# A gated mix of linear attention and a GLU on one core: half of the gates' logits taken from the transposed x, the rest behind the query folds; sums stored by rows; diagonals built at the load

## The chip, the core and the metric

The kernel runs on one core of a Trainium2 chip. TensorE (PE) multiplies, VectorE (DVE) and ScalarE (ACT) work on data in on-chip memory, SyncE (SP) and GpSimd (POOL) here only issue DMAs. The metric is the time of one execution on the device in microseconds (us); three runs of a kernel give a median.

## The reference: what is computed

```python
x = A_x                                            # 2048 x 1024, float32
g = sigmoid((x * gate_w).sum(-1, keepdims=True))   # the gates: one logit per token
a = _A_ref(x, A_wqkv, A_w_phi, A_wo)               # linear attention, 32 heads of 32
b = _B_ref(x, B_w_gate, B_w_up, B_w_down)          # (gelu(x @ w_gate) * (x @ w_up)) @ w_down
return g * a + (1 - g) * b
```

In `_A_ref` queries and keys go through a per-head 32x32 map `w_phi`; the features are softmax(p) and softmax(-p) side by side, 64 to a head. Two sums over all keys, `kv` (features times values) and `z` (features alone), finish the key side; each query then gives `num / den`, and `wo` follows.

## The kernel before, in words

**Tiling.** Everything is float32, split into a high and a low part (`high` on ACT, `low` on DVE), and each product is made of three passes on PE. Large products use a seven-product block scheme (Strassen-Winograd form): sums of quarters of x and of weights are formed first, on DVE. Tokens come in two halves of 1024. The first pool runs 79 units of seven steps; a step is twelve 128x512 matmuls (`product`, L748, L755). First come seven units for keys and values of half 1, then half 0's keys and values, half 0's gate, up and query columns, and from `second_turn` on the same columns for half 1, with kept weights. The last stage (L1456) multiplies by `wo` and `w_down`.

**Folds.** `w_phi` is folded into the key and query weights: `key_fold` and `query_fold` multiply a 128-row piece of the weights by a block-diagonal 128x128 matrix that `diagonal` (L473) builds on DVE. The eight query folds (L944 to L974) load `wqT` into one of two buffers (`into`), build the diagonal in one of two places, put eight products, which the trace shows as 16 matmuls, between two steps as a "filler", copy the result on ACT and store it from POOL to `wq_fold`.

**The sums of x for half 0.** `late_sums` (L246) loads chunk `kc` of two token blocks of the transposed x (`x_load`, rows `kc` and `kc + 4` of eight groups of 128 features), makes four sums on DVE (`x_sums`) and stores them from POOL in `xs_late`. Chunks 1 and 3 belong to `first_part` and use the `pts` tile (`raw`); chunks 0 and 2 belong to `second_part` and use `extra[2]` and `extra[3]`, two of four parts of the tile `work`.

**The gates.** `gates` (L919) runs in `second_part`, after its late sums: gate_w is broadcast to all rows (`extra[0]`), the 16 blocks of 128 rows of x are loaded in turn into `extra[2]` and `extra[3]` (SP, L925), one DVE instruction with an accumulator makes each block's logits (L933), and a sigmoid on ACT and two small DVE instructions follow (L938 to L941). After that the same three parts take the pieces of x for the first turn (`pieces`, `x_convert`; L276). They go in fixed order through the three buffers, and only when they are through may the features start (`entered`); `first_part`'s query folds must be done too (`prepared`).

**Features, finish, attention.** 32 jobs of `features` (L979) load keys and values, transpose (L1001), form the softmax and add to `kv` through a filler (L1052). `finish` (L1068) reads the 32 partial sums, adds, transposes and stores them in `sums_of` (L1108) with four DMAs on SP; `attention` (L1124) then works on the queries in the background of the units.

**The order of the work** is written by a planner inside the kernel. Each stream of work is a generator that yields requests (engine, length, ready time, due step); `run` (L191) picks, ahead of each PE step, what can start before it, the earliest start first, then the earliest due step. Lengths and landing times are constants (`LAND` 5.0, `STORE` 4.5, a step 2.73). The order it finds is fixed in each engine's queue: at run time an instruction waits in its queue for its data, and all behind it wait too. A DMA on SP waits in SP's queue likewise.

Of the kernel before, what the change touches and what calls it, by code (L numbers as in the profile page):

```python
# [8 lines left out]
F32 = mybir.dt.float32  # L9
F32R = mybir.dt.float32r  # L10
AF = mybir.ActivationFunctionType
OP = mybir.AluOpType
# [4 lines left out]
P = 128  # L17
KC = D // P
NF = DF // P
NG = H // 4  # L20
# [11 lines left out]
def tile_gated_mix(ctx: ExitStack, tc: tile.TileContext, x, xT, wkT, wqT, wv, w_phi, wo,  # L32
# [100 lines left out]
    with tc.tile_pool(name="xa", bufs=1) as xa, tc.tile_pool(name="fp", bufs=1) as fp, \  # L133
# [112 lines left out]
        def late_sums(half, which, r1, r2, free):  # L246
            for kc in which:
                end = yield SYN, LAND + 2.0, free, INF
                x_load(half, kc, r1, r2)
                steps = x_sums(r1, r2)  # L250
                for part in (0.75, 0.75, 1.5):
                    end = yield VEC, part, end, now[0] + 8
                    next(steps, None)
                for k, t in enumerate((r2[:, BLK:], r1[:, :BLK], r2[:, :BLK], r1[:, BLK:])):
                    nc.gpsimd.dma_start(xs_late[half][k][:, kc, :], t)
                free = end + STORE + 1.0
            return free
# [191 lines left out]
                    f"p ({' '.join(names)}) -> p {' '.join(names)}", **dict(zip(names[1:], shape[1:])))  # L449

        tails = fp.tile([P, 256], F32, name="tails")

        def new_f(dtype):
            return fp.tile([P, 1024], dtype, tag="f", name="f", bufs=1)
# [24 lines left out]
        work = new_quarter(0, 0).rearrange("p a b c -> p (a b c)")  # L479
        gated = [[work.bitcast(F32)[:, (2 * j + m) * BLK:(2 * j + m + 1) * BLK] for m in range(2)] for j in range(2)]  # L480
        extra = [work.bitcast(F32)[:, 1024 * k:1024 * k + 1024] for k in range(4)]
        raw_in = work[:, 3072:]
        EARLY = 12
        spare = new_weight(F32).rearrange("p i a b -> p (i a b)")
# [191 lines left out]
        highs((1, 2), (1, 3))  # L676
        for k, _ in stages[:4]:
            held[k] = 0.0

        raw_free = [INF, INF, INF]  # L680

# [208 lines left out]
        def first_part():  # L890
            yield SYN, 0.0, lambda: raw_free[2], INF
            raw = xa.tile([P, 2, 2 * BLK], F32, tag="pts", name="raw", bufs=1)
            pts_free[0] = INF
            into = [raw[:, 0], raw[:, 1]]
            free = yield from late_sums(0, (1, 3), *into, 0.0)
            yield from query_folds(into, free)
            pts_free[0] = max(folded[g] for g in range(NG))
            places[0].blocks = new_f(F32R).rearrange("p (b c) -> p b c", c=P)
            prepared[0] = 0.0

        def second_part():
            free = yield from late_sums(0, (0, 2), extra[2], extra[3], lambda: folded["k"])
            free = yield from gates([extra[2], extra[3]], extra[0], free)
            ends_of = []

            def turned(end):
                ends_of.append(end)
                if len(ends_of) == 2:
                    entered[0] = max(ends_of)
            start(pieces(first_turn, 0, extra[2], (0, 4), free, turned))  # L910
            start(pieces(first_turn, 0, extra[3], (1, 5, 9, 11, 13), free, turned))
            start(pieces(first_turn, 0, extra[0], (2, 6, 8, 10, 12), free))
            start(ring_pieces(first_turn, 0, (3, 7)))
# [2 lines left out]
            p = places[0]  # L916
            return max(p.free, p.attended, other_free[0])

        def gates(into, gw, free):  # L919
            yield SYN, LAND, free, INF  # L920
            nc.sync.dma_start(gw, gate_w[None, :].to_broadcast([P, D]))
            landed = []

            def load(c, at):
                nc.sync.dma_start(into[c % 2], x[c * P:(c + 1) * P, :])  # L925
                landed.append(at + 5.2)

            for c in range(2):
                load(c, free + c)
            for c in range(S // P):  # L930
                end = yield VEC, 1.25, lambda c=c: landed[c], now[0] + 6
                s = into[c % 2]
                nc.vector.scalar_tensor_tensor(s, s, 1.0, gw, op0=OP.mult, op1=OP.mult, accum_out=logit[:, c:c + 1])  # L933
                if c + 2 < S // P:
                    load(c + 2, end)
            out = end
            end = yield SCA, 0.3, end, now[0] + 6, "sigmoid"
            nc.scalar.activation(g_a, logit, AF.Sigmoid)  # L938
            yield VEC, 1.2, end, now[0] + 6
            nc.vector.tensor_scalar(g_b, g_a, -1.0, 1.0, OP.mult, OP.add)  # L940
            nc.vector.tensor_scalar(g_n, g_a, 1.0, -1.0, OP.mult, OP.add)  # L941
            return out

        def query_folds(into, free):  # L944
            free = [free] * 2
            for g in range(NG):
                s = into[g % 2]
                landed = yield SYN, LAND + 6.0, lambda: free[g % 2], INF
                nc.sync.dma_start(s, wqT[g])
                free[g % 2] = INF  # L950
                end = yield VEC, 0.3, landed, now[0] + 6
                bp = query_diagonals[g % 2]
                diagonal(bp, g)
                fillers.append((lambda end=end: max(end, misc_free[0]), query_fold(g, s, bp, free), 1.9))
            yield SYN, 0.0, lambda: max(free), INF

        def query_fold(g, s, bp, free):
# [110 lines left out]
        def finish(p):  # L1068
            landed = yield SYN, LAND + 7.0, lambda: max(max(kept), place_free(), v_free[0], pts_free[0]), INF
            z, other = tails[:, :64], tails[:, 64:P]  # L1070
            p.second(new_f(F32)[:, :1024])
            raw = xa.tile([P, 2, 2 * BLK], F32, tag="pts", name="raw", bufs=1)
            pts_free[0] = INF
            chunks, total = [*p.wide, raw[:, 0], raw[:, 1]], raw_in.bitcast(F32)
            for c, t in enumerate(chunks):
                nc.sync.dma_start(t.rearrange("p (u n) -> p u n", n=2 * P), kv_parts[:, 4 * c:4 * c + 4])
            soon = lambda: now[0] + 3
            yield VEC, 1.1, 0.0, soon()
            nc.vector.tensor_tensor(z, z, other, OP.add)
            for at in (32, 96):  # L1080
                nc.vector.tensor_copy(other[at - 32:at], z[at:at + 32])
            nc.vector.tensor_tensor(z[:96], z[:96], other[:96], OP.add)
            nc.vector.tensor_copy(other[:32], z[64:96])
            nc.vector.tensor_tensor(z[:32], z[:32], other[:32], OP.add)
            nc.vector.transpose(other[:32], z[:32])
            for q in range(4):
                nc.gpsimd.dma_start(sums_of[32 * q:32 * q + 32, 1].rearrange("b u d -> u b d"),
                                    other[16 * (q % 2):16 * (q % 2) + 16, 32 * (q // 2):32 * (q // 2) + 32]
                                    .unsqueeze(1).to_broadcast([16, 32, 32]))
            for c, t in enumerate(chunks):  # L1090
                end = yield VEC, 0.85, landed + 1.5 * c, now[0] + 12
                for h in range(2):
                    rows = slice(64 * h, 64 * h + 64)
                    e = t[rows].rearrange("p (u e s h f) -> p e h u s f", u=4, e=2, s=2, h=2)[:, :, h]
                    nc.vector.tensor_tensor(total[rows, 256 * c:256 * c + 256].rearrange("p (u s f) -> p u s f", u=4, s=2),
                                            e[:, 0], e[:, 1], OP.add)
            pts_free[0] = end
            end = yield VEC, 1.27, end - SIGNAL, soon()
            nc.vector.transpose(p.wide[0], total)
            moved = yield SCA, 2.2, end, soon()  # L1100
            rows = [slice(64 * h, 64 * h + 32) for h in range(2)]
            for h in range(2):
                nc.scalar.activation(p.wide[1][rows[h]], p.wide[0][64 * h + 32:64 * h + 64], AF.Copy)
            end = yield VEC, 2.5, moved, soon()
            for h in range(2):
                nc.vector.tensor_tensor(p.wide[1][rows[h]], p.wide[0][rows[h]], p.wide[1][rows[h]], OP.add)
                for s in range(2):
                    nc.sync.dma_start(sums_of[64 * s + 32 * h:64 * s + 32 * h + 32, 0],  # L1108
                                      p.wide[1][rows[h]].rearrange("p (u s d) -> p s u d", s=2, d=32)[:, s])
            yield VEC, 1.6, end - SIGNAL, soon()  # L1110
            for h in range(4):
                for q in range(4):
                    nc.vector.tensor_copy(g_at[32 * h:32 * h + 32, :, q], g_a[32 * q:32 * q + 32, :])
            p.parts = {n: raw_in.bitcast(F32)[:, at:at + size] for n, at, size in
                       (("kz", 0, 128), ("kb", 128, 128), ("mm", 256, 32), ("st", 288, 96))}
            p.free = sums_ready[0] = end + STORE + 8.0

        def load_query(p, half, g, j):
            nc.sync.dma_start(p.e[:64], heads["q"][half][g][j].rearrange("(w r) t -> r w t", w=2))
# [425 lines left out]
```

## Time and profile before

| | us |
|---|---|
| median of three runs | 2341.13 (2337.79 to 2342.32) |
| the profiled execution | 2341.17 |
| its span, first to last instruction | 2339.3 |
| PE busy | 2315.9 (99%) |
| DVE busy | 1811.5 (77%) |
| ACT busy | 1111.0 (47%) |
| POOL busy | 380.2 (16%) |

Rows of the timeline give start, length, engine, line, operation and what is written from what; in brackets the idle time before it and what ended it. `SPq` rows are DMA issues in SP's queue: their length is how long they held the queue, waits between them included where several are merged (x2). A row of windows gives a stretch, its length, then busy time and number of instructions of PE, PEld (weight loads), DVE, ACT and POOL, then PE's granted clock, the share of DMA engines busy and GB/s. Tiles go by their names in the program: `x` covers `work` and its parts, `f` the constants and later other uses, `tyz` and `wgu` weights, `misc` the folds' results.

### The profile page before, as it was taken

Reading aid. Unit: us, or ns where it says so; the run is one execution under the profiler, and the core shown is the slowest. Engines: PE = TensorE matmul, PEld = TensorE weight load, DVE = VectorE, ACT = ScalarE, POOL = GpSimd, SP = SyncE. Lnnn points to the kernel's source line nnn. Section 1 sums busy time; section 2 is a strip of 40 time slices with the busy share of each in tenths; the row PEclk is TensorE's granted clock in tenths of the full one; section 3 lists DMA queues with packets and bytes.
Section 4 is the critical chain, followed back from the end, with each engine's and each line's share of the span. In section 5 each row is a group of like instructions: output and inputs, shape, how many; then the busy total and the mean of one; then the engine's idle time right before and its main releaser. Section 6 shows DMA issues by size and latency. Waiting matters only on the chain.

```text
span 2339.3 us, 29314 instructions
## 1 busy us (share of the span) xinstructions
PE 2315.9 (99%) x10408; PEld 1921.2 (82%) x10408; DVE 1811.5 (77%) x2402; ACT 1111.0 (47%) x1496; POOL 380.2 (16%) x646
## 2 busy tenths in 40 slices
PE   8999999999999999999999999999999999999999
PEld 7778888888888888878888888888888888888887
DVE  7655898888988888878899888872674868867774
ACT  6435555565555656555566655652433332223221
POOL 3211111111222122222323222232000000000000
PEclk9999999999999999999999999999999999999999
DMA  9888548888889889898888888886784767978773
GB/s 340 298 286 293 162 150 291 308 307 312 315 297 330 302 285 318 285 301 245 249 239 261 233 246 251 236 252 212 275 283 153 262 241 267 325 255 314 267 264 134
DMA packets 238610, 622.33 MB, mean 266 GB/s; under 512 B 31936, under 2 KB 69568, under 8 KB 222592
## 3 DMA queue, kind: packets, MB, share of 16 engines
q1 hardware_dynamic: 149360, 308.47, 40.4%
q0 software_dynamic: 87904, 311.73, 39.9%
q8 instruction: 82, 1.34, 0.2%
q14 instruction: 64, 0.52, 0.1%
q10 hardware_dynamic: 1200, 0.26, 0.1%
HBM read 413.79 MB, written 206.57 MB: 265 GB/s over the span
## 4 chain that ended last, share of the span: by engine, by line
PE 92%; DMA 4%; issue 2%; DVE 1%; ACT 1%; POOL 0%; SPq 0%; DVEq 0%; POOLq 0%; ACTq 0%
PE po L1456 29%; PE a L755 25%; PE c L755 17%; PE b L755 9%; PE p L755 8%; PE misc L1052 1%; PE misc L1211 1%; DMA stage<-wk 1%; DMA raw<-in_xT 1%; DMA stage<-in_wv 1%; DMA x<-in_xT 0%; PE misc L962 0%; DMA stage<-xs 0%; DMA wk<-stage 0%; DMA xs<-x 0%
## 5 line engine op out<-in xcount | busy, mean ns | idle before, releaser
L1456 PE MATMUL po<-tw,wgu 128*128 128x512 f32 x1344 | 309.8, 389 | 0.0
L1456 PEld LDWEIGHTS po<-tw,wgu 128*128 128x128 f32 x1344 | 252.3, 188 | 52.3
L116 ACT ACTIVATE wgu<-stage 128x1024 fp32r<-128x1024 f32 x130 | 137.5, 1058 | 305.2 <-PE po L1456 227.8
L119 DVE TENSOR_TENSOR wgu<-stage,wgu 128x1024 fp32r<-128x1024 f32 x130 | 158.6, 1220 | 127.8 <-ACT wgu L116 127.7
L755 PE MATMUL c<-x,tyz 128*128 128x512 f32 x948 | 228.8, 390 | 4.1 <-ACT c L772 3.4
L755 PE MATMUL b<-s,tyz 128*128 128x512 f32 x948 | 229.6, 391 | 2.3 <-ACT b L783 2.3
L755 PE MATMUL a<-s,v 128*128 128x512 f32 x948 | 228.3, 389 | 1.5 <-DVE s L119 0.8
L755 PE MATMUL c<-x,wgu 128*128 128x512 f32 x948 | 228.7, 390 | 0.9 <-DVE x L119 0.6
L755 PE MATMUL a<-x,wgu 128*128 128x512 f32 x948 | 228.6, 390 | 0.8 <-DVE h L739 0.8
L755 PE MATMUL a<-s,tyz 128*128 128x512 f32 x948 | 228.4, 389 | 0.2 <-DVE tyz L119 0.2
L755 PE MATMUL p<-s,tyz 128*128 128x512 f32 x948 | 228.1, 389 | 0.0
L755 PEld LDWEIGHTS c<-x,tyz 128*128 128x128 f32 x948 | 177.3, 188 | 42.6 <-ACT c L772 5.0
L755 PEld LDWEIGHTS b<-s,tyz 128*128 128x128 f32 x948 | 178.0, 189 | 39.8 <-ACT b L783 3.1
L755 PEld LDWEIGHTS a<-s,v 128*128 128x128 f32 x948 | 177.8, 188 | 38.9 <-ACT s L116 1.2
L755 PEld LDWEIGHTS a<-x,wgu 128*128 128x128 f32 x948 | 178.1, 188 | 38.5 <-DVE h L739 1.2
L755 PEld LDWEIGHTS c<-x,wgu 128*128 128x128 f32 x948 | 177.1, 188 | 37.9 <-DVE x L119 1.0
L755 PEld LDWEIGHTS a<-s,tyz 128*128 128x128 f32 x948 | 177.4, 188 | 37.0 <-DVE tyz L119 0.7
L755 PEld LDWEIGHTS p<-s,tyz 128*128 128x128 f32 x948 | 177.4, 188 | 36.4
L1456 PE MATMUL po<-tw,wl 128*128 128x512 f32 x672 | 156.9, 389 | 0.0
L1456 PE MATMUL po<-tyz,wgu 128*128 128x512 f32 x672 | 155.2, 389 | 0.0
L1456 PEld LDWEIGHTS po<-tw,wl 128*128 128x128 f32 x672 | 126.2, 188 | 26.2
L1456 PEld LDWEIGHTS po<-tyz,wgu 128*128 128x128 f32 x672 | 126.2, 188 | 26.2
(442 smaller groups left out, 3561.0 us busy)
## 6 DMA issues: line engine op xcount, KB each, us to landing
stage<-lm SPq DMA_DIRECT2D x98, 512.0 KB, 3.6
sr<-in_w_down SPq DMA_DIRECT2D x84, 512.0 KB, 5.8
sl<-lm SPq DMA_DIRECT2D x70, 512.0 KB, 4.5
lm<-h POOLq DMA_DIRECT2D x112, 256.0 KB, 4.5
stage<-in_w_gate SPq DMA_DIRECT2D x28, 512.0 KB, 7.0
stage<-in_w_up SPq DMA_DIRECT2D x28, 512.0 KB, 5.8
stage<-la SPq DMA_DIRECT2D x28, 512.0 KB, 4.8
sr<-in_wo SPq DMA_DIRECT2D x20, 512.0 KB, 5.8
```

Source lines behind the costliest of these rows:

```text
L116: nc.scalar.activation(dst, src, AF.Copy)
L119: nc.vector.tensor_tensor(dst, src, dst_h.bitcast(F32), OP.subtract)
L755: nc.tensor.matmul(dst, w[:, h, 4 * part + kc, :], xq[:, e, kc, :], start=first and kc == 0 and i == 0, stop=kc == 3 and i == 2, skip_grou ...
L1052: nc.tensor.matmul(po[:, :2 * P], blocks[:, b], pts[:, b].rearrange("p e q f -> p (e q f)"), start=b == 0, stop=b == 7, skip_group_check=True)
L1211: nc.tensor.matmul(po[s], kbs[:, s].rearrange("p a b -> p (a b)"), pts[:, q, s, :], start=q == 0, stop=q == 1)
L1456: nc.tensor.matmul(ps[c], ls[:, a, m, c * P:(c + 1) * P], rs[:, e, m], start=opens and m == 0 and j == 0, stop=closes and m == 1 and j == 2)
```

## The change

`late_sums` now also makes dots: for each loaded block (token block `j`, features `kc` and `kc + 4`) two DVE instructions add feature times gate weight into `dots`, 128 partitions by 1024 tokens, which is `extra[0]`. The gate weights come as columns (`gate_columns`, 128 x 8) by a new DMA on SP at the end of the prologue. `second_part` then calls `first_logits`: `dots` is transposed in 32x32 blocks, reduced, moved across partitions by 16 small copies and reduced again to the first eight columns of `logit`. The other eight blocks of rows are done by `second_logits`, called in `first_part` behind the query folds, with the folds' buffers and a new `f` tile; its loads are requested at most one in two steps. The sigmoid follows there, and `prepared` is set after it.

In `query_folds` the diagonal is requested at once after the load is issued, no longer when the load has landed; the filler keeps waiting for the landing. In `finish` the last addition writes `total` in the order of the stored rows, so that a store's row is one run of 512 elements instead of 16 runs of 32, and the planner counts the sums as ready 3 us after `STORE` in place of 8.

```diff
@@ late_sums @@
                 x_load(half, kc, r1, r2)
+                for r, j in ((r1, 1), (r2, 0)):
+                    yield VEC, 1.5, end, now[0] + 8
+                    for a in range(2):
+                        at, c = slice(BLK * j, BLK * j + BLK), kc + 4 * a
+                        s, gate_c = r[:, BLK * a:BLK * a + BLK], gate_columns[:, c:c + 1]
+                        if j in dotted:
+                            nc.vector.scalar_tensor_tensor(dots[:, at], s, gate_c, dots[:, at], op0=OP.mult, op1=OP.add)
+                        else:
+                            nc.vector.tensor_scalar(dots[:, at], s, gate_c, 0.0, OP.mult, OP.add)
+                            dotted.add(j)
                 steps = x_sums(r1, r2)
...
+        gate_columns, dotted = tails[:, P:P + 8], set()
...
+        dots = extra[0]
...
+        nc.sync.dma_start(gate_columns, gate_w.rearrange("(c p) -> p c", p=P))
@@ first_part @@
             yield from query_folds(into, free)
-            pts_free[0] = max(folded[g] for g in range(NG))
+            free = max(folded[g] for g in range(NG))
+            end = yield from second_logits([into[1], new_f(F32)], into[0], free)
+            pts_free[0] = end
             places[0].blocks = new_f(F32R).rearrange("p (b c) -> p b c", c=P)
+            yield from gates(end)
             prepared[0] = 0.0
@@ second_part @@
-            free = yield from gates([extra[2], extra[3]], extra[0], free)
+            free = yield from first_logits(extra[2], extra[3], free)
...
+        def first_logits(t, r, free):
+            end = yield VEC, 1.27, free, now[0] + 8
+            nc.vector.transpose(t, dots)
+            end = yield VEC, 1.25, end - SIGNAL, now[0] + 8
+            nc.vector.tensor_reduce(r[:, :32], t.rearrange("p (b i) -> p b i", i=32), AX.X, OP.add)
+            end = yield VEC, 2.2, end - SIGNAL, now[0] + 8
+            parts = r[:, 32:64].rearrange("p (a c) -> p a c", a=4)
+            for a in range(4):
+                for q in range(4):
+                    nc.vector.tensor_copy(parts[32 * q:32 * q + 32, a], r[32 * a:32 * a + 32, q:32:4])
+            nc.vector.tensor_reduce(logit[:, :8], parts.rearrange("p a c -> p c a"), AX.X, OP.add)
+            return end
+
+        def second_logits(into, gw, free):
             yield SYN, LAND, free, INF
             nc.sync.dma_start(gw, gate_w[None, :].to_broadcast([P, D]))
+            landed, first, end = [], now[0] + 1, 0.0
+            for c in range(8, 16):
+                at = yield SYN, LAND, lambda: max(free if c < 10 else end, begun(first + 2 * (c - 8))), INF
                 nc.sync.dma_start(into[c % 2], x[c * P:(c + 1) * P, :])
+                landed.append(at)
+                if len(landed) == 2:
+                    end = yield VEC, 1.25, landed.pop(0), now[0] + 6
+                    dot(into[(c - 1) % 2], gw, c - 1)
+            end = yield VEC, 1.25, landed.pop(0), now[0] + 6
+            dot(into[1], gw, 15)
+            return end
@@ query_folds @@
-                end = yield VEC, 0.3, landed, now[0] + 6
+                end = yield VEC, 0.3, 0.0, now[0] + 6
                 bp = query_diagonals[g % 2]
                 diagonal(bp, g)
-                fillers.append((lambda end=end: max(end, misc_free[0]), query_fold(g, s, bp, free), 1.9))
+                fillers.append((lambda end=max(end, landed): max(end, misc_free[0]), query_fold(g, s, bp, free), 1.9))
@@ finish @@
             for h in range(2):
-                nc.vector.tensor_tensor(p.wide[1][rows[h]], p.wide[0][rows[h]], p.wide[1][rows[h]], OP.add)
+                by_s = [w[rows[h]].rearrange("p (u s d) -> p s u d", s=2, d=32) for w in p.wide]
+                out = total[rows[h]].rearrange("p (s u d) -> p s u d", s=2, d=32)
+                nc.vector.tensor_tensor(out, by_s[0], by_s[1], OP.add)
                 for s in range(2):
                     nc.sync.dma_start(sums_of[64 * s + 32 * h:64 * s + 32 * h + 32, 0],
-                                      p.wide[1][rows[h]].rearrange("p (u s d) -> p s u d", s=2, d=32)[:, s])
+                                      out[:, s])
...
-            p.free = sums_ready[0] = end + STORE + 8.0
+            p.free = sums_ready[0] = end + STORE + 3.0
```

`dot` is the old loop's instruction (L933), and the new `gates` holds only the sigmoid and the two instructions after it.

More of the change, by code (lines that the diff above doesn't have):

```diff
@@ L917, in place_free, with dot, gates @@
             return max(p.free, p.attended, other_free[0])
-        def gates(into, gw, free):
+        def first_logits(t, r, free):
[11 more added lines that the diff above has]
+        def second_logits(into, gw, free):
             yield SYN, LAND, free, INF
             nc.sync.dma_start(gw, gate_w[None, :].to_broadcast([P, D]))
-            landed = []
-            def load(c, at):
+            landed, first, end = [], now[0] + 1, 0.0
+            for c in range(8, 16):
+                at = yield SYN, LAND, lambda: max(free if c < 10 else end, begun(first + 2 * (c - 8))), INF
                 nc.sync.dma_start(into[c % 2], x[c * P:(c + 1) * P, :])
[L926 to L936, printed above, removed]
+                landed.append(at)
[5 more added lines that the diff above has]
+            return end
+        def dot(s, gw, c):
+            nc.vector.scalar_tensor_tensor(s, s, 1.0, gw, op0=OP.mult, op1=OP.mult, accum_out=logit[:, c:c + 1])
+        def gates(end):
             end = yield SCA, 0.3, end, now[0] + 6, "sigmoid"
@@ L941, in gates @@
             nc.vector.tensor_scalar(g_n, g_a, 1.0, -1.0, OP.mult, OP.add)
-            return out
         def query_folds(into, free):
@@ L1105, in finish @@
             for h in range(2):
-                nc.vector.tensor_tensor(p.wide[1][rows[h]], p.wide[0][rows[h]], p.wide[1][rows[h]], OP.add)
+                by_s = [w[rows[h]].rearrange("p (u s d) -> p s u d", s=2, d=32) for w in p.wide]
+                out = total[rows[h]].rearrange("p (s u d) -> p s u d", s=2, d=32)
+                nc.vector.tensor_tensor(out, by_s[0], by_s[1], OP.add)
                 for s in range(2):
-                    nc.sync.dma_start(sums_of[64 * s + 32 * h:64 * s + 32 * h + 32, 0],
-                                      p.wide[1][rows[h]].rearrange("p (u s d) -> p s u d", s=2, d=32)[:, s])
+                    nc.sync.dma_start(sums_of[64 * s + 32 * h:64 * s + 32 * h + 32, 0], out[:, s])
             yield VEC, 1.6, end - SIGNAL, soon()
```

## The prediction

> **What bounds the kernel now.** I read the page first, for span and chain.
>
> ```profile
> span 2339.3 us, 29314 instructions
> PE 92%; DMA 4%; issue 2%; DVE 1%; ACT 1%; POOL 0%; SPq 0%; DVEq 0%; POOLq 0%; ACTq 0%
> ```
>
> TensorE (PE) is the bound and works on nearly all the time, so an edit that adds or removes no matmul can gain only where PE stands still or runs at a lower clock. The profiled execution took 2341.17 us, 1.9 us around its span, and the median of the runs is 2341.13: the sum is made against 2341.2. Next, PE's waits in three stretches: 100 to 200, 200 to 1000 and 1000 to 1100 us (after 1100 there are none). Columns: total, times, longest.
>
> ```profile
> PE misc L962 <- issue: 3.9, 1, 3.9
> PE c L755 <- ACT c L772: 3.0, 2, 2.7
> PE a L755 <- DVE h L739: 0.8, 1, 0.8
> PE b L755 <- ACT b L783: 0.5, 1, 0.5
> ...
> PE a L755 <- DVE s L119: 0.8, 1, 0.8
> PE a L755 <- ACT s L116: 0.7, 1, 0.7
> PE c L755 <- DVE x L119: 0.7, 1, 0.7
> ...
> PE b L755 <- ACT b L783: 1.8, 1, 1.8
> PE c L755 <- DVE x L119: 0.6, 1, 0.6
> ```
>
> These 12.8 us are nearly all that can be won. Two stalls also cost clock (windows; PEclk is the number before the DMA share):
>
> ```profile
> 172.00:178.00 6.00, 5.94 (x27) 5.55 (x28) 5.96 (x9) 1.98 (x4) 0.38 (x1) 0.72 0.59 215
> 1020.60:1028.00 7.40, 7.33 (x25) 5.90 (x26) 4.53 (x5) 3.59 (x6) 3.62 (x6) 0.77 0.82 261
> ```
>
> **Part 1: the gates leave the early stretch.** The old loop sends 16 loads of x rows through SP's queue; each waits there for the dot product that frees its buffer, and the weight loads stand behind it. SP's queue, what SP waited for (60 to 260 us), and the vector engine (DVE) and PE in time:
>
> ```profile
> 157.82 5.87 SPq L925 DMA_DIRECT2D x<-in_x  x2
> 163.79 0.56 SPq L43 DMA_DIRECT2D stage<-wk  x1
> ...
> SPq L925 <- DVE x L933: 45.2, 13, 7.9
> ...
> 170.34 0.69 DVE L97 TENSOR_TENSOR stage<-stage 128x512 f32<-128x512 f32 x1 [5.59 <-DMA stage<-wk]
> 171.68 0.28 DVE L474 TENSOR_TENSOR f<-f 128x128 f32<-128x128 f32 x1
> ...
> 172.06 3.65 PE L962 MATMUL misc<-f,raw 128*128 128x128 f32 x16 [3.87 <-issue]
> 186.46 1.95 PE L962 MATMUL misc<-f,raw 128*128 128x128 f32 x16
> ```
>
> This is the 3.9 us stall from end to end: the x-row loads held SP for 5.87 us, the weight load went out at 163.79, DVE stood 5.59 us for it, the fold's diagonal (L474) was queued behind on DVE, and PE behind the diagonal. The change cuts it twice: the loads are gone from there, and the diagonal is issued at the load instead of at the landing. Removed: 3.87 of idle, and 3.65 − 1.95 = 1.70 of slow clock: **−5.6**. The 0.8, 0.5 and 0.3 (3.0 − 2.7) of the same stretch are work of the same queues behind dots and late weights: **−1.6**. What is late next there is the landing of wqT itself, which is requested when its buffer is free and not changed in size.
>
> The eight dots and eight loads that are left, with one broadcast of gate_w, now follow the folds, at some 190 to 240 us by the planner's spacing of two steps (5.4 us) a load. There SP carries the first-turn pieces of x, and DVE their conversions. A load that waits for a late dot would again hold weights and pieces; between 0 and the 5.6 of the stall above. The new loop asks for a load after the dot that frees its buffer, so I take the row nearest to this, two small stalls of 0.8: **+1.6**.
>
> **Part 2: the first-turn pieces start earlier.** Their three buffers were the gates'.
>
> ```profile
> 183.71 0.43 SPq L276 DMA_DIRECT2D stage<-xs  x1
> ...
> 229.85 1.48 SPq L276 DMA_DIRECT2D x<-xs  x2
> ```
>
> The first piece went out just after the last dot, the last two only at 229.85, and PE then waited 0.8 + 0.7 + 0.7 for conversions. Free sooner (the planner lets the first piece go eleven steps ahead of its half's first unit), the chain through the buffers gets ahead of its uses: **−2.2**; at worst 0. The first half of the logits needs a transpose, two reductions and 16 small copies on DVE after the late sums; at most some 7 us (1.25 each for transpose and reduction by the first row below, 16 copies of 32 rows by at most the 0.28 of L474), in place of 16 × 1.22 = 19.5 of dots taken from the same stretch: 0.
>
> ```profile
> L1001 DVE STREAM_TRANSPOSE x<-x x32: 1235/1245/1247, 241.9 to 948.5; 128x1024 f32<-128x1024 f32 x32
> L933 DVE SCALAR_TENSOR_TENSOR x<-x x16: 1212/1219/1226, 120.9 to 181.4; 128x1024 f32<-128x1024 f32 x16
> ```
>
> **Part 3: finished sums by rows.** SP's queue at the second turn, the stores' own durations in ns (least, median, most), and the chain's pieces on PE:
>
> ```profile
> 1001.67 6.90 SPq L1108 DMA_DIRECT2D sums<-f  x4
> 1008.68 2.55 SPq L276 DMA_DIRECT2D stage<-in_xT  x1
> ...
> L1108 SPq DMA_DIRECT2D sums<-f x4: 319/1970/2509, 1001.7 to 1006.1; - x4
> ...
> 1020.66 4.30 PE b L755 x12
> ```
>
> Each store writes 32 rows in 16 pieces of 128 bytes; after the first, which found the queue empty, each held it about 2 us, and the load of the x piece behind them another 2.55. Stored as 32 runs of 2 KB, all four should take about the least, 4 × 0.32 = 1.3 instead of 6.90: the piece goes out 5.6 us earlier. PE's wait for its conversion (0.6) and for ACT's copy behind the next pieces (1.8) are both shorter than 5.6 and should go, with 1.4 of slow clock (4.30 for a group of twelve that takes 2.88 in the row of 92.32 below): **−3.8**. DVE's addition only changes its access order, at the same count.
> The Trainium skill (TensorE: Matmul & The Clock Gate, Part 1: The HAM clock gate) says that PE falls to half clock after an idle window of about 3.4 us, windows that run freely. Here 0.77 was granted after 0.6 + 1.8 of idle in two parts; by the rule on the length alone part 3 would be worth −2.4 and the sum 1.4 less (an estimate). The row decides.
>
> **Part 4: the dots beside the late sums.** Four chunks get four instructions each of 128x512 on DVE, 16 in all, ahead of each chunk's sums.
>
> ```profile
> L240 DVE TENSOR_TENSOR x<-x x2: 691/692/692, 88.2 to 108.2; 128x512 f32<-128x512 f32 x2
> 60.00:100.00 40.00, 39.63 (x181) 32.53 (x181) 27.78 (x37) 16.55 (x25) 11.71 (x21) 1.00 0.89 285
> ...
> 90.87 1.22 DVE L119 TENSOR_TENSOR tyz<-stage,tyz 128x1024 fp32r<-128x1024 f32 x1
> 92.32 2.88 PE L755 MATMUL a<-s,tyz 128*128 128x512 f32 x12
> ...
> 97.02 1.24 SPq L233 DMA_DIRECT2D x<-in_xT  x2
> 98.31 0.60 SPq L43 DMA_DIRECT2D stage<-in_wv  x1
> ...
> 108.26 0.63 ACT L116 ACTIVATE v<-stage 128x512 fp32r<-128x512 f32 x1 [6.02 <-DMA stage<-in_wv]
> ```
>
> By L240's 0.69 that is 2.76 us a chunk, 11 in all, into a stretch whose DVE is busy 27.78 of 40 (a mean, that hides queues). The low half of the z weights ended at 92.09 for a matmul at 92.32: slack 0.2. If the dots go ahead of it, PE waits about 2.76 − 0.2 = 2.5; there are two such chunks (88.2 and 108.2 us), so the loss is up to 5.0. The planner takes the earlier due time among ready work, and dots have eight steps. On the other side, chunks end 3 us later, so the x load of 97.02 may fall behind the wv load of 98.31, whose late landing held ACT for 6.02 and, behind it, the copy for which PE stood the 2.7 above: that would be −2.7. Between −2.7 and +5.0 I take one late z: **+2.5**.
>
> **Part 5: the column load of gate_w.** 1,024 elements of 4 bytes, each alone in DRAM, at 43.6 us on SP.
>
> ```profile
> L43 SPq DMA_DIRECT2D stage<-in_wv x1: 1480/1480/1480, 43.6 to 43.6; - x1
> ...
> DMA to landing us min/median/max: 9.8/9.8/9.8
> ...
> 57.42 1.05 ACT L116 ACTIVATE wgu<-stage 128x1024 fp32r<-128x1024 f32 x1
> ```
>
> From above: twice the pieces of a sums store at 2.5, so 5.0 of the queue; from below 0.3. The weight load behind it landed at 43.6 + 9.8 = 53.4 and was used at 57.42, so 4.0 is covered: between 0 and +1.0. I take 0.
> The Trainium skill (DMA: Bandwidth & Descriptors, Rules for kernel authors) speaks against this edit: a last dimension that is not contiguous becomes one descriptor per element. By it the upper end, +1.0, would hold (an estimate), and the sum be −8.1.
>
> **Not on the path.** Features start when both the pieces and now the logits are done, so a few us later or as before; their end and attention's leave slack: 1600:1650 has DVE at 15.10 of 50 before the last stage. The sums are counted ready 5 us sooner: nothing waits there.
>
> ```profile
> 1600.00:1650.00 50.00, 50.00 (x222) 41.44 (x221) 15.10 (x18) 12.88 (x19) 8.41 (x14) 1.00 0.54 175
> ```
>
> Sum: −5.6 − 1.6 + 1.6 − 2.2 − 3.8 + 2.5 = −9.1, so 2341.2 − 9.1 = **2332**.
>
> **Rivals.** PE's matmuls of the query folds, first and last:
>
> ```profile
> L962 PE MATMUL misc<-f,raw x128: 270/275/485, 117.1 to 213.5; 128*128 128x128 f32 x128
> ```
>
> (a) The SP hold comes back: an x-row load of the second half waits for a late dot, with weights behind it. For it: 45.2 us of such waits in the old loop. Against: half the loads, issued after the dots. It costs 5.6 in place of 1.6, so −5.1: 2336.
> (b) The stores by rows don't help, since the finish has moved away from the second turn, or the pieces wait for ring buffers anyway: −9.1 + 3.8 = −5.3, 2336. For it: the planner's order is made anew. Against: the first transpose of the features at 241.9 is near where I expect the new one.
> (c) Slower: the features start late. Their start now waits for eight loads at two steps each, 14 steps or 38 us (14 × 2.7) behind the last fold's store. If the folds don't speed up (the last was at 213.5), that is past 251, and the finish with its reads, stores and DVE work falls on the second turn's conversions. From a delay of some 20 us the 3.8 isn't won and, by two more stalls like that one, 7.6 is lost: −9.1 + 3.8 + 7.6 = +2.3, 2343.5, and +6.1 with a third.
> (d) Better: z is never late, the wv load passes the x load, the x rows never hold SP: −9.1 − 2.5 − 2.7 − 1.6 = −15.9, 2325.
>
> **Chances.** Forecast 0.43 (2329.5 to 2335), (a) 0.16, (b) 0.13, (c) 0.18, (d) 0.10. About 0.2%, 4.7 us, is what a measurement of this kernel tells from no change. (a) and (b) lie at −5.1 and −5.3, on that edge, half each way: faster 0.43 + 0.10 + 0.15 = 0.68. (c) starts at +2.3; two thirds of it beyond +4.7: slower 0.12, and the same 0.20. The range goes from (d) to (c), 2325 to 2344.
>
> **What would show it.** The wait of L962 on issue gone, no L925 in SP's queue between 117 and 183 us; SP's four sums stores under 2 us and clock 1.00 after 1020; no wait of L755 on x or s conversions near 231. Wrong, if L755 waits for L119 near 90 or 112 us (part 4), if the new loads hold SP for 5 us (a), if the first features' transpose is past 260 us (c).

## The result, and the profile after

The changed kernel takes 2325.78 us (median of six runs, 2323.88 to 2328.37); the kernel before, run beside it, 2340.66 (2337.01 to 2342.32). The ratio is 0.9938, with a 95% interval of 0.9926 to 0.9951: 14.5 us less, between 11.5 and 17.3. The forecast was 9.1 us less, 2332; the time lies at the good end of the range, 0.8 us inside it and next to rival (d)'s 2325. The profiled execution took 2328.37, the longest of the six, and has a span of 2326.6, 12.7 less than before's 2339.3.

The page after, span and chain:

```profile
span 2326.6 us, 29294 instructions
PE 94%; DMA 3%; DVE 1%; ACT 0%; issue 0%; SPq 0%; DVEq 0%; ACTq 0%
```

The chain runs over PE for 94% where it was 92%. PE's waits in the changed kernel, the stretch of 50 to 100 us first and that of 300 to 600 us behind it; from 100 to 300 and from 600 on there are none:

```profile
PE c L768 <- ACT c L785: 2.2, 2, 1.9
PE c L768 <- ACT c L789: 0.3, 1, 0.3
PE a L768 <- DVE tyz L119: 0.2, 1, 0.2
...
PE a L768 <- ACT c L789: 0.9, 1, 0.9
PE a L768 <- DVE h L742: 0.7, 1, 0.7
```

Of the 12.8 us of waits that the prediction listed, none is left; 3.5 us stand elsewhere (1.9 + 0.9 + 0.7). The stretch of the old gates' loop, in windows of the kernel before and then of the changed one (PE busy is the second number):

```profile
117.00:185.00 68.00, 62.35 (x304) 51.87 (x303) 41.86 (x66) 24.37 (x39) 8.68 (x16) 0.97 0.82 286
```

```profile
117.00:185.00 68.00, 68.00 (x350) 58.08 (x350) 37.97 (x63) 30.19 (x45) 12.45 (x23) 1.00 0.72 248
172.00:178.00 6.00, 6.00 (x35) 5.17 (x34) 2.15 (x3) 4.00 (x7) 1.08 (x2) 1.00 0.62 241
1000.00:1050.00 50.00, 50.00 (x226) 41.55 (x225) 29.94 (x57) 22.55 (x31) 15.81 (x26) 1.00 0.96 309
```

PE went from 304 matmuls in these 68 us to 350, without a gap and at full clock, and the second turn (1000 to 1050 us, 47.55 busy before) has no gap either. SP's queue in the changed kernel, at the first pieces, the late rows of x, and the second turn:

```profile
44.45 0.48 SPq L691 DMA_DIRECT2D tails<-in_gate_w  x1
...
94.22 0.37 SPq L43 DMA_DIRECT2D stage<-in_wv  x1
...
107.23 0.88 SPq L233 DMA_DIRECT2D x<-in_xT  x2
...
156.45 1.93 SPq L286 DMA_DIRECT2D x<-in_xT  x2
...
210.31 1.19 SPq L954 DMA_DIRECT2D raw<-in_x  x1
...
1006.41 1.56 SPq L286 DMA_DIRECT2D stage<-xs  x2
...
1013.85 0.32 SPq L1105 DMA_DIRECT2D x<-kvp  x1
...
1039.94 2.01 SPq L1139 DMA_DIRECT2D sums<-x  x4
```

Four things are to be seen. The column load held SP for 0.48 us. The wv load (94.22) now goes ahead of the x load (107.23). The first piece of x goes out at 156, not at 184. And the finish stands in another place: it reads its parts at 1013.85, behind the last piece of the second turn (1006.41), and stores at 1039.94; before, the stores went out at 1001.67, in the middle of the pieces. The first features are later to match (first and last start of the transposes; before 241.9 to 948.5):

```profile
L1030 DVE STREAM_TRANSPOSE x<-x x32: 1234/1245/1246, 261.9 to 991.4; 128x1024 f32<-128x1024 f32 x32
```

### The profile page after: what moved, and what is told of

Read it like the earlier page. It is cut to its first block, busy times and chain, and to the rows that moved or that the text cites. A ratio compares the mean times of both kernels' runs of the same rounds, so it can differ in the third digit from the quotient of the medians.

```text
span 2326.6 us, 29294 instructions
## 1 busy us (share of the span) xinstructions
PE 2313.7 (99%) x10408; PEld 1921.9 (83%) x10408; DVE 1816.0 (78%) x2421; ACT 1108.1 (48%) x1494; POOL 379.7 (16%) x646
## 4 chain that ended last, share of the span: by engine, by line
PE 94%; DMA 3%; DVE 1%; ACT 0%; issue 0%; SPq 0%; DVEq 0%; ACTq 0%
PE po L1486 29%; PE a L768 26%; PE c L768 18%; PE b L768 9%; PE p L768 9%; PE misc L1241 1%; PE misc L1081 1%; DMA raw<-in_xT 1%; DMA stage<-in_wv 1%; PE misc L991 1%; DMA stage<-in_wkT 0%; DMA stage<-wk 0%; DMA stage<-wq 0%; DMA wgu<-in_wkT 0%; DMA stage<-in_w_gate 0%
```

## The experiments

Ratios are to the kernel before, run on the same chip, with a 95% interval; 0.001 is 2.3 us.

### One part at a time, and one part undone

**Stores by rows alone**, in the kernel before, the planner's times untouched:

```diff
-                nc.vector.tensor_tensor(p.wide[1][rows[h]], p.wide[0][rows[h]], p.wide[1][rows[h]], OP.add)
+                by_s = [w[rows[h]].rearrange("p (u s d) -> p s u d", s=2, d=32) for w in p.wide]
+                out = total[rows[h]].rearrange("p (s u d) -> p s u d", s=2, d=32)
+                nc.vector.tensor_tensor(out, by_s[0], by_s[1], OP.add)
                 for s in range(2):
                     nc.sync.dma_start(sums_of[64 * s + 32 * h:64 * s + 32 * h + 32, 0],
-                                      p.wide[1][rows[h]].rearrange("p (u s d) -> p s u d", s=2, d=32)[:, s])
+                                      out[:, s])
```

> The kernel before with the finished sums stored by rows and nothing else; the planner's times are left as they were, so its order is the same. Theory A (the stores held the pieces of x at the second turn): the four stores take 1.3 to 2.0 us of SP's queue instead of 6.9, PE's waits of 1.8 and 0.6 near 1017 us and the slow clock behind them go, about -3.8 us against the kernel before. Theory B (the pieces wait for ring buffers or for ACT anyway): the stores are short, but the waits stay, within 1 us of before.

Measured: 2338.53 us against 2339.55, ratio 0.9994 (0.9985 to 1.0003). Its stores in SP's queue, and the window that had the stall:

```profile
1001.26 3.08 SPq L1110 DMA_DIRECT2D sums<-x  x4
...
1012.00:1020.60 8.60, 8.60 (x40) 7.12 (x39) 5.50 (x5) 5.63 (x8) 1.70 (x4) 1.00 0.83 262
```

In this profile theory A holds, 6.9 us have become 3.1 and PE has no gap. The times show only 1.0 us, which is no difference that can be told, and the 3.8 that theory A expected lies outside the interval (−3.5 to +0.7). The second profile of the kernel before, further down, says why.

**Stores by pieces in the changed kernel:** the same lines the other way round.

> The changed kernel with the old stores of the sums (16 pieces of 128 bytes a row), all else as changed. Its finish comes at 1039 us, after the pieces of the second turn. If the stores by rows carried the gain at the second turn, 3.8 us come back against the changed kernel. If the later place of the finish carried it, the stores hold SP's queue for 7 us where nothing urgent is behind them, and the time is within 1 us of the changed kernel (some 15 us under the kernel before).

Measured: 2324.6 us, ratio 0.994 (0.9928 to 0.9953), the same as the changed kernel. PE has no wait from 900 to 1100 us. So in the changed kernel the stores by rows gain nothing that can be told; the later finish is enough by itself. And the stores by pieces were quick there (durations in ns):

```profile
L1137 SPq DMA_DIRECT2D sums<-f x4: 303/399/481, 1035.7 to 1037.3; - x4
```

These are the same 16 pieces of 128 bytes a row that took up to 2509 ns before. What held SP at 1001 us was not their shape alone, but also what else was under way at the second turn.

**The diagonals at the load alone**, in the kernel before:

```diff
-                end = yield VEC, 0.3, landed, now[0] + 6
+                end = yield VEC, 0.3, 0.0, now[0] + 6
...
-                fillers.append((lambda end=end: max(end, misc_free[0]), query_fold(g, s, bp, free), 1.9))
+                fillers.append((lambda end=max(end, landed): max(end, misc_free[0]), query_fold(g, s, bp, free), 1.9))
```

> The kernel before with the query folds' diagonals requested at the load and nothing else. If PE's 3.9 us wait was for the diagonal alone, it goes with its 1.7 us of slow clock: -5.6 us. If the x-row loads in SP's queue are the cause of more than that, the waits of 0.8, 0.5 and 0.3 stay, and the weights that were late at 170 us make the next step wait (the low part of z is late instead): between -1 and -4 us.

Measured: 2343.95 us against 2339.55, ratio 1.0026 (1.0015 to 1.0037): slower, where both readings had expected a gain. The wait for the diagonal is gone, but other waits of that stretch have grown:

```profile
156.94 3.01 PE L755 MATMUL a<-x,wgu 128*128 128x512 f32 x12 [2.09 <-DVE h L739]
...
160.79 2.02 PE L962 MATMUL misc<-f,raw 128*128 128x128 f32 x16 [0.84 <-DMA raw<-in_wqT]
...
181.84 4.42 PE L755 MATMUL b<-s,tyz 128*128 128x512 f32 x12 [2.99 <-ACT b L783]
```

**The diagonals at the landing in the changed kernel**, the same two lines undone:

> The changed kernel with the diagonals requested at the landing as before. If the x-row loads were what made the diagonal late, it is early enough here too: within 1 us of the changed kernel. If the request at the load is needed, one or more folds wait again, some 4 to 6 us slower than the changed kernel.

Measured: 2331.83 us, ratio 0.9967 (0.9955 to 0.9979): 0.0029 over the changed kernel, some 7 us. Yet PE has no wait at all from 100 to 200 us. It waits further on:

```profile
228.40 5.06 PE L768 MATMUL a<-s,v 128*128 128x512 f32 x11 [3.53 <-DVE s L119]
...
1072.61 3.02 PE L768 MATMUL a<-x,wgu 128*128 128x512 f32 x12 [2.06 <-DVE h L742]
...
1455.67 3.03 PE L768 MATMUL a<-x,wgu 128*128 128x512 f32 x12 [1.02 <-DVE h L742]
...
1483.58 3.04 PE L768 MATMUL c<-x,tyz 128*128 128x512 f32 x12 [1.08 <-ACT c L785]
```

So the diagonals at the load were not what freed 140 to 200 us. What they give in the changed kernel lies further on: at 228 us the low half of a piece stood on DVE behind a wait for a wv load, the features start at 278.9 in place of 261.9, and three more waits lie behind the second turn. That these come from the order that the planner finds with later folds was not tried apart.

### What in the gates' loop made PE wait

**Without the loop:** the kernel before, its broadcast, loads and dots taken out (every gate 0.5).

```diff
-            yield SYN, LAND, free, INF
-            nc.sync.dma_start(gw, gate_w[None, :].to_broadcast([P, D]))
...
-            for c in range(S // P):
...
+            end = yield VEC, 0.1, free, now[0] + 6
+            nc.vector.memset(logit, 0.0)
```

> The kernel before without the gates' loop: no broadcast, no loads of x rows, no dots; the logits are set to zero, so every gate is 0.5 and the output differs from the reference's by that. All else is as before (diagonals at the landing, stores by pieces). This is the price of the loop where it stood. If the chain of loads and dots in that stretch makes all of PE's waits of 117 to 240 us, they go, and the time is -9 to -14 us against the kernel before: the changed kernel then has nearly the whole of it. If the waits have another cause (the late weights themselves, the diagonals at the landing), 3 us of idle or more stay between 117 and 240 us, and the gain is under 6 us.

Measured: 2331.85 us against 2338.78, ratio 0.9968 (0.9955 to 0.9981): 7.5 us less, between 4.4 and 10.5. Two rows of PE, one of SP's queue, one of DVE, and the window:

```profile
113.70 4.61 PE L755 MATMUL c<-x,tyz 128*128 128x512 f32 x12 [3.67 <-ACT c L772]
...
231.97 2.79 PE L755 MATMUL a<-s,v 128*128 128x512 f32 x11 [1.09 <-DVE s L119]
...
157.98 1.54 SPq L276 DMA_DIRECT2D x<-in_xT  x2
...
228.23 0.69 DVE L97 TENSOR_TENSOR stage<-stage 128x512 f32<-128x512 f32 x1 [2.83 <-DMA stage<-in_wv]
...
117.00:185.00 68.00, 68.00 (x348) 57.99 (x348) 27.44 (x38) 30.60 (x45) 9.71 (x18) 0.99 0.61 215
```

The loop made all of PE's waits between 117 and 185 us, and the gain agrees with the 7.2 us of the prediction's first part; the 9 to 14 us expected for all waits up to 240 us did not come. DVE's time for the dots does not explain the waits by itself: DVE is busy for 41.86 us of this stretch in the kernel before and for 37.97 in the changed kernel, where PE has no gap. The DMA engines' share fell as well, from 0.82 to 0.61 here and to 0.72 in the changed kernel; what that did was not tried apart, but the changed kernel's second turn runs without a gap at 0.96.

The first piece of x goes out at 157.98 us here, almost as early as in the changed kernel, and PE still waited at 232 us: the piece's low half stood on DVE behind weights that had waited 2.83 us for a wv load. So pieces that start early are not enough to end that wait.

The stall near 112 us stays, and so do 1.8 us at 232 to 241 and 1.0 at the second turn: the changed kernel, which still does half of the loop elsewhere, is faster than this one by 0.003, and these are the places where.

**The same loads from another queue:** GpSimd in place of SP, in the kernel before.

```diff
-                nc.sync.dma_start(into[c % 2], x[c * P:(c + 1) * P, :])
+                nc.gpsimd.dma_start(into[c % 2], x[c * P:(c + 1) * P, :])
```

> The kernel before with the 16 loads of x rows in the gates issued by GpSimd in place of SP; the same bytes, the same dots on DVE at the same planned times. If SP's queue held by those loads is the cause of PE's waits at 140 to 200 us, the weight loads go out in time and these waits (5.6 us of idle in the profile before, 1.7 of slow clock) go: -5 to -7 us. If the cause is DVE's time for the dots or the DMA engines' load, they stay: within 1.5 us. A loss is possible where GpSimd's stores of results now wait behind a load: +2 us or more, with ACT or DVE waiting for the three h buffers.

Measured: 2341.77 us against 2339.34, ratio 1.001 (1.0001 to 1.0019). Nothing is won. What DVE waited for from 110 to 190 us in the kernel before, and then what DVE and GpSimd waited for here, and one fold:

```profile
DVE x L933 <- DMA x<-in_x: 13.0, 7, 5.4
DVE stage L97 <- DMA stage<-wk: 10.6, 2, 5.6
```

```profile
DVE x L933 <- DMA x<-in_x: 26.4, 11, 9.0
DVE stage L97 <- DMA stage<-wk: 1.1, 1, 1.1
...
POOL x L925 <- DVE x L933: 32.5, 12, 6.2
...
145.15 2.02 PE L962 MATMUL misc<-f,raw 128*128 128x128 f32 x16 [1.47 <-issue]
```

SP is free of the loads here, and DVE hardly waits for wk any more (1.1 us for 10.6). So the hold on SP's queue that the prediction described was there. But GpSimd now stands 32.5 us for dots and DVE 26.4 us for the loads of x rows, where it stood 13.0, with the folds' diagonals in line behind: the one for the fold at 145.15 was built at 144.76, right behind a dot that had waited 2.48 us for its load. The chain of load and dot over two buffers made the issuing queue wait, SP's or GpSimd's, and DVE's queue both times. Moving its loads to GpSimd doesn't help; taking it out of the stretch does.

**The dots alone**, in the kernel before, beside the old loop (the 16 instructions and the column load of the change; the logits still come from the loop):

```diff
                 x_load(half, kc, r1, r2)
+                for r, j in ((r1, 1), (r2, 0)):
+                    yield VEC, 1.5, end, now[0] + 8
...
+        nc.sync.dma_start(gate_columns, gate_w.rearrange("(c p) -> p c", p=P))
```

> The kernel before with the column load of gate_w and the 16 dot instructions beside the late sums; the logits still come from the old gates with all 16 loads of x rows (the dots are made and not used). My prediction's part 4 as run: the stall of 1.9 us near 91 us comes (ACT's copy behind v, whose weights land late because SP was held by the x loads) with up to 1.7 us of slow clock, and the one of 2.7 us near 111 us goes, since the x load falls behind the wv load: between -2 and +1.5 us against the kernel before; all stalls of 140 to 240 us stay. Rival: the dots take DVE from the folds and dots that follow, and the stalls of 140 to 180 us grow: +3 us or more.

Measured: 2345.18 us against 2340.25, ratio 1.002 (1.0012 to 1.0029). SP's order at the x load, and PE:

```profile
94.84 0.37 SPq L43 DMA_DIRECT2D stage<-in_wv  x1
...
106.72 0.88 SPq L233 DMA_DIRECT2D x<-in_xT  x2
...
213.97 4.11 PE L768 MATMUL a<-s,tyz 128*128 128x512 f32 x11 [3.49 <-DVE s L119]
...
235.40 2.79 PE L768 MATMUL c<-x,tyz 128*128 128x512 f32 x11 [2.61 <-DVE x L119]
```

The flip that the prediction offered as its lower bound is there: the wv load passes the x load, and there is no stall near 91 or 112 us. The dots themselves made no wait beside the late sums. Yet the kernel is 2.8 to 6.8 us slower, which only the rival had expected, and by another way than the rival's: the waits of 117 to 185 us shrank, from 5.7 to 1.9 us, and 10.1 us of waits stand at 196 to 243, nearly all for conversions of pieces. The old loop's loads start later (129.81 us, 117.24 before), and so do the pieces behind it (the last at 234.24, 229.85 before). I read the price as this delay; it was not tried apart.

**The column load**, alone in the kernel before:

```diff
+        nc.sync.dma_start(gate_columns, gate_w.rearrange("(c p) -> p c", p=P))
```

> The kernel before with only the column load of gate_w (1,024 elements of 4 bytes) on SP; nothing reads it. If it is hidden, the time is within 1 us and the first loads behind it land as before. If its 1,024 pieces slow the DMA engines or hold SP, the wv loads behind it land 2 to 5 us later and PE waits near 57 to 67 us: +1 to +4 us.

Measured: 2341.77 us against 2340.25, ratio 1.0005 (0.9996 to 1.0014), no difference that can be told. And in the changed kernel, issued from ACT's queue at the start:

```diff
-        nc.sync.dma_start(gate_columns, gate_w.rearrange("(c p) -> p c", p=P))
...
+        nc.scalar.dma_start(gate_columns, gate_w.rearrange("(c p) -> p c", p=P))
```

> The changed kernel with the column load moved from SP's queue at 44 us to ACT's queue at the start, behind the two loads of w_phi. If that load is why SP is 1.5 to 2 us later at the late sums (67.66 against 65.90 us) and so why v lands late, the stall of 1.9 us near 91 us and its slow clock go: -2 to -4 us against the changed kernel. If the stall comes from the dots' time on DVE, it stays: within 1 us.

Measured: 2326.3 us, ratio 0.994 (0.9926 to 0.9953), as the changed kernel. Its profile has 0.7 us at 92 us where the changed kernel's has 1.9, but the kernel with stores by pieces, whose queues are the same there, had 1.4, so this wait differs from run to run.

### Which stalls are there in every execution

**The kernel before, profiled again.**

> The kernel before, profiled a second time, to see which of its stalls are there in every execution. If the stall of 3.9 us at 168 us and the two of 1.8 and 0.6 near 1017 us belong to the program, they are there again within 0.5 us, with the slow clock; if they hang on the landing of single DMAs, one or more of them is missing or twice as long.

Measured: 2339.55 us. PE's waits from 100 to 200 us, and from 1000 to 1100 us:

```profile
PE misc L962 <- issue: 3.6, 1, 3.6
PE c L755 <- ACT c L772: 1.7, 2, 0.8
PE a L755 <- DVE h L739: 0.6, 1, 0.6
...
PE b L755 <- ACT b L783: 0.9, 1, 0.9
```

The fold's stall belongs to the program (3.6 and 3.9). The one near 112 us was 0.8 in this execution, 2.7 in the first and 3.7 in the kernel without the loop; those of the second turn were 0.9 in all, with full clock (49.00 of 50 us busy), against 2.4 and some 1.8 of slow clock in the first. The stores held SP's queue for 6.1 us this time too. Five more of the kernels here keep the old stores in that place (the diagonals alone, GpSimd's loads, the dots alone, the column load alone, no loop): the stores held SP for 5.9 to 6.7 us in each, PE waited 0.9 to 1.4 us, and its clock stayed full. So the hold is there each time, but the execution from which the prediction took part 3 is the only one of seven with a stall of 2.4 us and a slow clock behind it. That is why the rows alone show so little in the times.

### The place of the finish

The eight late loads of the changed kernel, planned one in a step, and one in four steps:

```diff
-                at = yield SYN, LAND, lambda: max(free if c < 10 else end, begun(first + 2 * (c - 8))), INF
+                at = yield SYN, LAND, lambda: max(free if c < 10 else end, begun(first + (c - 8))), INF
...
+                at = yield SYN, LAND, lambda: max(free if c < 10 else end, begun(first + 4 * (c - 8))), INF
```

> The changed kernel with the eight late loads of x rows planned at most one a step, not one in two. The logits are done some 15 to 19 us sooner, the features start near where they did in the kernel before (242 to 248 us) and the finish comes before or at the second turn. If the later finish is what the changed kernel gains at the second turn and the stores by rows do nothing there, a stall of 1 to 2.4 us comes back near 1000 us; if the stores by rows suffice, none does. Loads closer together may hold SP (rival a of the prediction): a wait of PE at 200 to 240 us. Within 3 us of the changed kernel either way.

Measured: 2327.04 us, ratio 0.9951 (0.9938 to 0.9964), near the changed kernel. The profiled execution is the longest of five, 2333.50 against 2324.80 to 2327.88 for the others. The features start at 256.1, the finish reads at 1000.41, among the pieces, and PE waited there:

```profile
1000.41 0.41 SPq L1105 DMA_DIRECT2D x<-kvp  x1
...
1002.41 1.76 SPq L1105 DMA_DIRECT2D raw<-kvp  x2
...
1020.58 0.79 PE L768 MATMUL c<-x,tyz 128*128 128x512 f32 x1 [3.57 <-ACT x L116]
...
1021.84 2.50 PE L768 MATMUL c<-x,tyz 128*128 128x512 f32 x5 [0.47 <-DVE x L119]
```

The stores, by rows, come only at 1033. With the finish among the pieces there can be a stall without them, though by the times one of this size is not the rule. ACT stood 8.59 us for the piece's load, which I read as the finish's reads sharing the way with it; that was not tried apart. At 200 to 240 us SP's loads made PE wait 0.1 us, so rival (a) has no ground even at this spacing.

> The changed kernel with the eight late loads planned one in four steps: the logits done 14 steps or 38 us later, the features start near 300 us and the finish near 1075 us. Rival (c) of the prediction gave a price of 7.6 us or more to a late start, by two stalls at the second turn and more behind it: +4 to +11 us against the changed kernel. If the background work has the slack that the low DVE share of 1600 to 1650 us (15 of 50) suggests, within 1.5 us.

Measured: 2336.37 us, ratio 0.9987 (0.9978 to 0.9996), 0.0049 or 11 us over the changed kernel. The second turn has no gap. The price is at the end of the units:

```profile
1635.64 0.50 PE L1241 MATMUL misc<-pts,stage 128*128 128x512 f32 x1 [2.69 <-ACT pts L116]
...
1636.99 1.35 PE L1241 MATMUL misc<-pts,stage 128*128 128x512 f32 x3 [0.85 <-DVE pts L119]
...
1642.24 13.69 PE L1486 MATMUL po<-tyz,wgu 128*128 128x512 f32 x48 [3.90 <-ACT h L1260]
...
1600.00:1650.00 50.00, 42.56 (x173) 33.90 (x172) 33.91 (x48) 25.24 (x34) 6.89 (x12) 0.90 0.59 193
```

The features started at 296.8, and the last attention is no longer done when the units end; the last stage waits for it. In the changed kernel this last product runs at 1611.63. So a start 20 us later than in the kernel before leaves no wait at the end of the units, and neither does one 37 us later (278.9, with the diagonals at the landing); one 55 us later costs 11 us.

## Why the prediction was right, and where it was not

The direction and the range held, the range by 0.8 us; the point was 5.4 us short (9.1 against 14.5). By its steps:

- **Part 1, the loop leaves (−7.2):** right in size. All waits of 117 to 185 us are gone, and the kernel without the loop gains 7.5 us (4.4 to 10.5). The way was told too narrowly. The prediction said that the change cuts the stall twice, at the loads and at the diagonal; the diagonal alone made the kernel slower, and in the changed kernel it is not what frees this stretch. And the hold on SP's queue is only one part of the cause: with the loads on GpSimd it is gone and nothing is won, since the chain of loads and dots then holds GpSimd's queue and DVE's.
- **The late rows (+1.6):** mis-sized. From 200 to 300 us there is no wait. The two small waits of the changed kernel near 482 and 514 us (1.6) are outside this step, and waits of the same kind show at the same units in other runs (0.6 and 0.6 in the second profile of before).
- **Part 2, the pieces start earlier (−2.2):** the waits of 231 to 239 us are gone and the first piece goes out at 156.45, as forecast, but the one does not follow from the other alone. The kernel without the loop sent its first piece at 157.98 and waited 1.8 us at 232 to 241; the changed kernel with the diagonals at the landing sent it at 156.45 and waited 3.5 us at 228. In both, a piece's low half stood on DVE behind weights that waited for a wv load, which the prediction did not count. The changed kernel and its four other variants have 0.1 us or less there, so more than chance is in it, but what it is was not tried apart.
- **Part 3, stores by rows (−3.8):** the step failed, though its place was right. The stall of the second turn went, but rows are not needed for that: with the old stores the changed kernel is as fast. It went because the finish moved: its stores went from 1001 to 1040 us, which the prediction held for a danger (rival c). By itself the edit takes the stall away in a profile and shows 1.0 us in the times, which can't be told from nothing. The term was mis-sized too, since the stall was 0.9 to 1.4 us, at full clock, in six profiles of seven. And the cost of a store was taken from its shape, while the same store took 0.3 to 0.5 us at another time.
- **Part 4, the dots (+2.5 taken, −2.7 to +5.0):** the wrong end. No low half of z was late. The wv load passed the x load, and the 2.7 us went, as the lower bound had it. What came instead is the wait of 1.9 near 92 us, for ACT's copy behind v, with a slow clock (twelve matmuls in 4.59 us where 2.88 is usual):

```profile
88.21 0.63 ACT L116 ACTIVATE v<-stage 128x512 fp32r<-128x512 f32 x1 [6.08 <-DMA stage<-in_wv]
...
91.78 4.59 PE L768 MATMUL c<-x,tyz 128*128 128x512 f32 x12 [1.87 <-ACT c L785]
```

  It differs from run to run (0 to 1.9 in the profiles of the changed kernel and its five variants), and the dots alone had none.
- **Part 5, the column load (0):** right; the upper bound of 5.0 us of SP's queue was ten times too high (0.48).
- **Rivals.** (a) did not come. (b) has its first half: the finish moved, but the stall left with it. (c) began, the features were 20 us late, at its point of decision, and nothing was lost; its price is real but stands at the end of the units, from a delay between 37 and 55 us. (d) has the outcome by most of its reasons (z never late, wv ahead of x, no hold by the late rows). That the time falls so near its 2325 is luck all the same: its sum holds 3.8 for the stores by rows, which gave nothing of that size, and nothing for the wait near 92 us.

The profiles account for the span: waits of PE are 10.6 us fewer (8.4 at 100 to 200 us, 2.2 at 200 to 300, 2.4 at the second turn, 1.2 in the first 50 us, where landings differ in every run; 1.8 more at 50 to 100 and 1.8 more at 300 to 600), and PE is busy 2.2 us less (2315.9 to 2313.7), for slow clock at 172 and 1022 us that is gone and some at 92 that is new. Together 12.8 of the 12.7. That is one execution of each kernel; the medians lie some 2 us further apart, and no profile shows where.

## What to carry to other kernels

A loop of load and use over two buffers, planned into queues that other work runs through, held that work by its own landings, from SP's queue as from GpSimd's; look for a stretch where nothing urgent stands behind it. A stall in one profile is one draw: profile the kernel twice before its whole size goes into a sum, above all where it hangs on a DMA that lands beside others; that a queue is held for 6 us each time does not say that PE pays for it each time. When an edit moves background work, find where that work must be done at the latest, and price the delay there, not at the next busy place.

## What the runs showed of the hardware that was not expected

- A load of 1,024 single elements of 4 bytes held SP's queue for 0.48 us and landed after 5.0 to 6.3 us; a store of 512 pieces of 128 bytes held it between 0.30 and 3.42 us, by the time at which it was issued.
- The same stall at the second turn, in two executions of one program, was 2.4 us with 0.77 of the clock behind it and 0.9 us at full clock: the longer wait cost nearly twice itself.
- The length of a wait alone did not decide the clock: after 1.87 us near 92 us in the changed kernel twelve matmuls took 4.59 us, and after 2.72 us near 112 us in the kernel before they took 3.04.
